# A fused forward and backward kernel on one core: the front's loads move from the SyncE queue to the GpSimd queue, and k is loaded in another order and in parts

## The chip, the cores and the metric

The kernel runs on 1 core of one Trainium2 chip. The core has five engines with queues of their own: TensorE (PE, with its weight loads PEld), VectorE (DVE), ScalarE (ACT), GpSimd (POOL) and SyncE (SP), and 16 DMA engines. Any of SP, ACT and POOL can issue a DMA. An instruction at the head of an engine's queue waits for its semaphores, and all behind it wait with it. The metric is the device time of one execution in microseconds; the median of several runs counts.

## The reference

One sequence of S = 2048 positions with D = 512 channels, F = 1376 hidden units, all bf16. The forward pass and the gradients of all inputs but `B_x` are computed.

```python
def _A_ref(q, k, v, shift_k, ssm_k, ssm_D):
    ks = shift_k.shape[-1]                      # 4
    k_pad = jnp.pad(k, ((0, 0), (ks - 1, 0), (0, 0)))
    k_shift = jnp.zeros_like(k)
    for t in range(ks):
        k_shift = k_shift + k_pad[:, t:t + S, :] * shift_k[:, ks - 1 - t][None, None, :]
    kv = k_shift * v
    ...                                         # y = kv * ssm_k, a long convolution by FFT of length 2 S
    y = y + kv * ssm_D[None, None, :]
    return q * y

def _B_ref(x, w_gate, w_up, w_down):
    ...
    return jnp.einsum("bsf,fd->bsd", g * u, w_down)

xn = _layernorm(A_q, axis=-1)
return A_q + _A_ref(xn, A_k, A_v, A_shift_k, A_ssm_k, A_ssm_D) + _B_ref(xn, B_w_gate, B_w_up, B_w_down)
...
_out, _vjp = jax.vjp(_f, ...)                   # outputs: _out and the gradients for grad_out
```

## The kernel before, in words

A position is 16 p + r: partition p holds R = 16 neighbouring rows r. Rows are worked on in eight chunks of two: chunk b is the rows 2b and 2b+1 of every partition, 128 x 2 x 512 bf16 or 256 KB. The long convolution is a Fourier transform written as matmuls with tables that the kernel makes itself (`Tables`), in two stages: `stage1` per row, then groups of 16 frequencies (`g_fwd`, `g_mul`, `g_inv`), then the inverse.

Two streams of work share the engines. `main()` is the gated layer: `ffn1(ch)` computes gate, up and the back-propagated hidden values of chunk ch (L509, L515), `yb(ch)` the two outputs (L545, L552) and adds the residual's x (`xb`, L540, used at L547). `side` is `front()` followed by `groups()`. A pacing counter takes a step of `side` after each piece of `main()`. The names in `tc.manual_schedule` and the priorities aside, the order on each engine is set by a scheduler when the program is built; at run time each engine goes through its own list in that order.

The front is what the change touches. For chunk b:
- `load_x(b)` loads x and the gradient: tiles `x_b` (4 buffers) and `go_b` (3 buffers), L300 and L305. x of chunk 5 takes the buffer of chunk 1, the gradient of chunk 4 that of chunk 1, and so on.
- `norm(b)` makes the layer norm in place: statistics and aggregates on VectorE (L323, L324), the root on ScalarE (L330), reciprocal and two rows on VectorE (L336, L339); `store_xn` writes it to memory (L347).
- `pre(b)` computes dy = gradient times xn (L380, one buffer), then ks, the sum of four shifted rows of k times the small kernel (L388, L390, L391; `ks_b` has 2 buffers and is stored at L396), and kv = ks times v (L398, in place in `v_b`, 2 buffers). dy and kv go through `stage1` (L367); ScalarE copies each result from PSUM to `fst` (L235), and L373 stores it.
- `kernel_spec()` does the same for the long kernel `ssk` in chunk 0's turn; there VectorE (L238) and ScalarE share the copies to `fst`.
- k lies in one tile `kh` of 19 rows a partition: rows 3 to 18 are the partition's own, rows 0 to 2 the three rows in front, which belong to the partition before. `load_k()` (L308) sets the first partition's front rows to zero on VectorE, loads the 2 MB of own rows, and then the front rows in two pieces (L311, L312). ks of chunk 0 reads the front rows first.

`late_loads()` calls `load_k()` and spreads the small kernel over the partitions; `front()` calls it after the first step. The tile `kh` lies where the tables' temporaries were, so it can be written when the last table has been read. Before that, the first loads (x and gradient of chunks 0 to 2, v of chunks 0 and 1, x of chunk 3, the weights) go out on SP; a part of the weights goes on ACT. In the kernel before every other load and store of the front is issued by SP too: SP's queue holds, in the scheduler's order, loads, the stores of xn, ks, fst, the hidden values `HDD`, and the DMA transposes (L491) that give `ffn1` its operands. GpSimd makes some of the tables and is then idle.

The buffers tie the loads to the work: a load into a buffer waits until the last reader of its former content is done, and stands in its queue meanwhile.

## Time and profile before

| what | value |
|---|---|
| runs | 487.74, 485.74, 487.5 us; median 487.5 |
| the profiled execution | 488.18 us, of which the span of the core is 486.3 |
| TensorE clock granted | 0.999 |
| DMA, whole span | 139.87 MB, 288 GB/s |
| stores of ks, issue to landing | 2.8 / 4.0 / 4.3 us (least, median, most) |
| loads of x (`x_b`) | 2.9 / 6.2 / 10.4 us |
| loads of the gradient (`go_b`) | 2.7 / 3.9 / 4.9 us |
| loads of v (`v_b`) | 3.1 / 4.6 / 10.2 us |
| loads of the residual's x (`xb`) | 2.8 / 3.1 / 3.9 us |

All five rows of loads and stores are of 256 KB each. In the page's tables a group of instructions stands as "busy us (x count)" per engine; in a timeline as start, duration, engine, line, operation, output<-input; in a list of waits as "who <- for whom: us in total, times, the longest". "SPq" is the queue of SP, that is the time in which it issues or waits; "issue" is time for which the profile shows no cause. In the table of stretches the columns are the stretch, its length, busy time and count of PE, PEld, DVE, ACT and POOL, the granted clock, the share of the DMA engines and GB/s. The front runs from about 25 to 120 us, the groups of frequencies from 130 to 300, the gradients of the weights and the last outputs from 300 on.

### The profile page before, as it was taken

Reading aid. Unit: us, or ns where it says so; the run is one execution under the profiler, and the core shown is the slowest. Engines: PE = TensorE matmul, PEld = TensorE weight load, DVE = VectorE, ACT = ScalarE, POOL = GpSimd, SP = SyncE. Lnnn points to the kernel's source line nnn. Section 1 sums busy time; section 2 is a strip of 40 time slices with the busy share of each in tenths; the row PEclk is TensorE's granted clock in tenths of the full one; section 3 lists DMA queues with packets and bytes.
Section 4 is the critical chain, followed back from the end, with each engine's and each line's share of the span. In section 5 each row is a group of like instructions: output and inputs, shape, how many; then the busy total and the mean of one; then the engine's idle time right before and its main releaser. Section 6 shows DMA issues by size and latency. Waiting matters only on the chain.

```text
span 486.3 us, 10468 instructions
## 1 busy us (share of the span) xinstructions
PE 468.3 (96%) x4293; PEld 314.7 (65%) x4335; DVE 340.6 (70%) x623; ACT 318.2 (65%) x354; POOL 14.0 (3%) x30
## 2 busy tenths in 40 slices
PE   8998998999999999999999999999999999999997
PEld 7876753647648547447447743576777787777875
DVE  7897979988274567686777856013266999999780
ACT  4976886859748778779779975366577535444141
POOL 8000000000000000000000000020000000000000
PEclk9999999999999999999999999999999999999999
DMA  8998998999997968968978279999999899699747
GB/s 273 375 417 307 311 247 295 353 317 330 318 296 228 267 204 259 288 199 244 296 238 268 91 288 322 387 319 309 332 349 408 285 374 413 194 266 224 207 153 249
DMA packets 105325, 139.87 MB, mean 288 GB/s; under 512 B 33307, under 2 KB 78784, under 8 KB 103742
## 3 DMA queue, kind: packets, MB, share of 16 engines
q1 hardware_dynamic: 103694, 137.84, 86.3%
q10 hardware_dynamic: 1584, 1.36, 1.0%
q8 instruction: 34, 0.56, 0.5%
q14 instruction: 13, 0.11, 0.1%
HBM read 68.45 MB, written 63.41 MB: 271 GB/s over the span
## 4 chain that ended last, share of the span: by engine, by line
PE 59%; DMA 17%; DVE 16%; SPq 3%; issue 2%; ACT 1%; ACTq 0%
PE pgu L509 13%; PE px L552 13%; PE pdh L515 6%; PE py L545 6%; PE pu L1031 6%; DMA hb<-HDD 4%; DMA Wg<-in_B_w_gate_dram 4%; DMA out_dram<-o 3%; PE ps L581 3%; PE pg L610 3%; PE pt L839 2%; PE pd L995 2%; PE pf L367 2%; DMA kh<-in_A_k_dram 2%; DVE dk L1086 2%
## 5 line engine op out<-in xcount | busy, mean ns | idle before, releaser
L552 PE MATMUL px<-WT,hd 128*128 128x512 bf16 (+1 forms) x339 | 78.6, 380 | 1.6 <-issue 1.4
L1031 PEld LDWEIGHTS <-xnC 128*128 128x128 bf16 x704 | 67.0, 98 | 8.9 <-issue 0.9
L552 PEld LDWEIGHTS <-hd 128*128 128x128 bf16 (+1 forms) x352 | 32.8, 98 | 44.2 <-issue 7.3
L1031 PE MATMUL pu<-natd,xnC 128*128 128x256 bf16 x512 | 58.5, 273 | 0.2 <-ACT nath L235 0.2
L235 ACT CAST GO<-pg 128x1024 bf16<-128x1024 f32 x48 | 46.2, 1015 | 13.4 <-issue 6.7
L597 DVE TENSOR_TENSOR T<-SP 128x2048 bf16<-128x2048 bf16 x24 | 29.3, 1222 | 34.8 <-ACT SP L235 34.8
L509 PE MATMUL pgu<-xt,Wu 128*128 128x256 bf16 (+1 forms) x352 | 53.2, 274 | 0.3
L235 ACT CAST SP<-ps 128x1024 bf16<-128x1024 f32 x48 | 46.5, 1027 | 10.3 <-PE ps L581 8.4
L509 PE MATMUL pgu<-xt,Wg 128*128 128x256 bf16 (+1 forms) x352 | 52.8, 273 | 0.3 <-DMA Wg<-in_B_w_gate_dram 0.3
L235 ACT CAST gu<-pgu 128x1024 bf16<-128x1024 f32 (+1 forms) x48 | 45.4, 945 | 11.8 <-PE pgu L509 11.3
L515 PE MATMUL pdh<-gt,WdT 128*128 128x256 bf16 (+1 forms) x352 | 46.9, 273 | 0.1
L509 PEld LDWEIGHTS <-Wu 128*128 128x128 bf16 (+1 forms) x352 | 32.9, 100 | 14.5 <-issue 9.9
L235 ACT CAST og<-pu 128x1024 bf16<-128x1024 f32 (+1 forms) x11 | 10.9, 993 | 46.8 <-PE pu L1031 28.8
L545 PE MATMUL py<-Wd,hd 128*128 128x512 bf16 (+1 forms) x168 | 40.1, 380 | 0.7 <-issue 0.5
L235 ACT CAST fst<-pf 128x1024 bf16<-128x1024 f32 x40 | 39.0, 1031 | 2.7 <-remote 1.4
L515 PEld LDWEIGHTS <-WdT 128*128 128x128 bf16 (+1 forms) x352 | 34.9, 100 | 5.4 <-ACT WdT L235 0.2
L235 ACT COPY natd<-pt 128x2048 bf16<-128x2048 bf16 x16 | 30.0, 1873 | 12.8 <-PE pt L839 12.8
L509 PEld LDWEIGHTS <-Wg 128*128 128x128 bf16 (+1 forms) x352 | 34.8, 100 | 4.2 <-DMA Wg<-in_B_w_gate_dram 0.6
L529 DVE TENSOR_TENSOR hd<-gu 128x512 bf16<-128x512 bf16 (+1 forms) x48 | 19.1, 397 | 20.7 <-ACT gu L235 20.7
L530 DVE TENSOR_TENSOR hd<-gu,dh 128x1024 bf16<-128x1024 bf16 (+1 forms) x48 | 30.8, 642 | 1.2 <-ACT dh L235 0.4
L545 PEld LDWEIGHTS <-hd 128*128 128x128 bf16 (+1 forms) x176 | 16.4, 98 | 20.5 <-issue 3.1
L597 DVE TENSOR_TENSOR U<-SP 128x2048 bf16<-128x2048 bf16 x24 | 29.2, 1217 | 0.0
(171 smaller groups left out, 696.1 us busy)
## 6 DMA issues: line engine op xcount, KB each, us to landing
HDD<-hd SPq DMA_DIRECT2D x35, 384.0 KB, 4.0
FD<-fst SPq DMA_DIRECT2D x24, 512.0 KB, 4.8
X<-FD SPq DMA_DIRECT2D x24, 512.0 KB, 5.2
GD<-GO SPq DMA_DIRECT2D x24, 512.0 KB, 3.5
g<-GD SPq DMA_DIRECT2D x12, 1024.0 KB, 8.9
hb<-HDD SPq DMA_DIRECT2D x8, 1344.0 KB, 8.4
bb<-BX SPq DMA_DIRECT2D x8, 512.0 KB, 8.6
BX<-bx SPq DMA_DIRECT2D x7, 512.0 KB, 3.9
```

The costliest lines, as they stand in the source:

```text
L235: nc.scalar.copy(o, i)
L367: nc.tensor.matmul(pf[:, c, :], lhsT=TB.W1[:, c, :], rhs=src[:, i, :], start=True, stop=not point)
L509: nc.tensor.matmul(pgu[:w, i, t, :], lhsT=W[:, c, f0:f0 + w], rhs=xt[:, :, c, :], start=(c == 0), stop=(c == NC4 - 1))
L515: nc.tensor.matmul(pdh[:w, i, :], lhsT=WdT[:, c, f0:f0 + w], rhs=gt[:, :, c, :], start=(c == 0), stop=(c == NC4 - 1))
L529: nc.vector.tensor_tensor(hd[:fw, fb0:fb0 + n, 0, :], gu[:fw, :n, 0, :], gu[:fw, :n, 1, :], op=ALU.mult)
L530: nc.vector.tensor_tensor(hd[:fw, fb0:fb0 + n, 1:3, :], gu[:fw, :n], dh[:fw, :n].unsqueeze(2).to_broadcast((fw, n, 2, 256)), op=ALU.mult)
L545: nc.tensor.matmul(py[:], lhsT=hd[:fw, fb, 0, ss], rhs=Wd[:fw, fb, :], start=(fb == 0), stop=(fb == NFB - 1))
L552: nc.tensor.matmul(px[:], lhsT=hd[:fw, fb, t, ss], rhs=W[:fw, fb, :], start=(t == 1 and fb == 0), stop=(t == 2 and fb == NFB - 1))
L581: nc.tensor.matmul(ps[32 * q:32 * q + 32, a, :], lhsT=TB.EF[64 * a:64 * a + 64, 4 * g + q, ri].rearrange("p k j -> p (k j)"), rhs=X[64 * a ...
L597: tt(W[:].rearrange("p c a d -> p c (a d)"), A[:, i:i + 1].rearrange("p c a d -> p c (a d)").to_broadcast((P, 2, 2 * D)), B[:].rearrange(" ...
L610: nc.tensor.matmul(pg[q // 2][64 * a:64 * a + 64, q % 2, :], lhsT=TB.EI[32 * q:32 * q + 32, 2 * g + a, yi].rearrange("p k c -> p (k c)"), ...
L1031: nc.tensor.matmul(pu[:, c, :, :fw], lhsT=xnC[:, r, cs(c)], rhs=nat_d(fb, r), start=(r == 0), stop=(r == R - 1))
```

## The change

Five loads are issued by GpSimd in place of SP: x from chunk 4 on, the gradient from chunk 3 on, v from chunk 2 on, all of k, and the residual's x in all eight chunks. The stores, the transposes and the first loads stay on SP. The zeros in `kh` are set by GpSimd in place of VectorE. k's front rows are issued first, then its own rows in two halves of 1 MB. `late_loads()` is called before the norm of chunk 2 in place of after it, which gives it an earlier place in the scheduler's order. What is computed and how many bytes move stay the same.

```diff
     def load_q(b):
         x = stp.tile([P, 2, D], BF, name="x_b", bufs=4)
-        nc.sync.dma_start(x[:], x_n[:, 2 * b:2 * b + 2, :])
+        (nc.sync if b < 4 else nc.gpsimd).dma_start(x[:], x_n[:, 2 * b:2 * b + 2, :])
         return x
 
     def load_go(b, x):
         go = stp.tile([P, 2, D], BF, name="go_b", bufs=3)
-        nc.sync.dma_start(go[:], go_n[:, 2 * b:2 * b + 2, :])
+        (nc.sync if b < 3 else nc.gpsimd).dma_start(go[:], go_n[:, 2 * b:2 * b + 2, :])
         XG[b] = (x, go)
 
     def load_k():
-        nc.vector.memset(ST["kh"][0:1, 0:3, :], 0.0)
-        nc.sync.dma_start(ST["kh"][:, 3:3 + R, :], k_n)
-        nc.sync.dma_start(ST["kh"][1:113, 0:3, :], k_n[0:112, R - 3:R, :])
-        nc.sync.dma_start(ST["kh"][113:128, 0:3, :], k_n[112:127, R - 3:R, :])
+        nc.gpsimd.memset(ST["kh"][0:1, 0:3, :], 0.0)
+        nc.gpsimd.dma_start(ST["kh"][1:113, 0:3, :], k_n[0:112, R - 3:R, :])
+        nc.gpsimd.dma_start(ST["kh"][113:128, 0:3, :], k_n[112:127, R - 3:R, :])
+        for r0 in range(0, R, R // 2):
+            nc.gpsimd.dma_start(ST["kh"][:, 3 + r0:3 + r0 + R // 2, :], k_n[:, r0:r0 + R // 2, :])
...
     def load_v(b):
         v = stp.tile([P, 2, D], BF, name="v_b")
-        nc.sync.dma_start(v[:], v_n[:, 2 * b:2 * b + 2, :])
+        (nc.sync if b < 2 else nc.gpsimd).dma_start(v[:], v_n[:, 2 * b:2 * b + 2, :])
         VB[b] = v
...
         xb = ybo.tile([P, 2, D], BF, name="xb", tag="xb", bufs=1)
-        nc.sync.dma_start(xb[:], x_n[:, 2 * ch:2 * ch + 2, :])
+        nc.gpsimd.dma_start(xb[:], x_n[:, 2 * ch:2 * ch + 2, :])
...
     def front():
         for b in range(8):
             if b == 0:
+                late_loads()
                 with tc.issue_after(TB.last.ins):
                     norm(2)
...
             yield
             if b == 0:
-                late_loads()
                 yield from kernel_spec()
```

In the order that is built from the changed source, TensorE's list differs from the one before only in some matmuls exchanged within the first 65 us. On VectorE the statistics, norm rows and products with k of the chunks stand earlier. On POOL the 27 DMAs stand in this order: k's front rows and halves; the residual's x of stage 0, the gradient of chunk 3, x of chunk 4; the gradient of chunk 4, x of chunk 5, v of chunk 2; the residual's x of stage 1, v of chunk 3; the gradient of chunk 5, x of chunk 6; the gradient of chunk 6, x of chunk 7, v of chunk 4; the gradient of chunk 7, v of chunks 5 and 6; the residual's x of stage 2, v of chunk 7; the residual's x of stages 3 to 7.

## The prediction

> **What bounds the kernel now.** I read first the page's busy shares and the table of stretches, then the waits of TensorE and VectorE, then the chain of waits, last the timelines where the chain leaves TensorE.

> ```profile
> PE 468.3 (96%) x4293; PEld 314.7 (65%) x4335; DVE 340.6 (70%) x623; ACT 318.2 (65%) x354; POOL 14.0 (3%) x30
> ...
> 40.00:50.00 10.00, 7.92 (x72) 6.21 (x71) 7.32 (x13) 7.33 (x10) 0.00 (x0) 1.00 0.91 287
> 70.00:80.00 10.00, 7.87 (x37) 3.48 (x36) 9.08 (x22) 5.86 (x10) 0.00 (x0) 1.00 0.80 258
> 80.00:100.00 20.00, 19.89 (x116) 11.34 (x117) 19.47 (x37) 12.89 (x17) 0.00 (x0) 1.00 0.94 329
> 100.00:120.00 20.00, 19.89 (x128) 12.51 (x129) 17.41 (x33) 16.21 (x20) 0.00 (x0) 1.00 0.92 323
> ```

> TensorE is the bound: 468.3 of 486.3 us, at full clock. Its 18.0 us of idle time lie mostly at the start, the end and two holes, in 40-50 and 70-80. From 80 to 120 it has 0.2 us left; VectorE is busy 36.9 of those 40. So the change can gain only what TensorE waits before 80, and it loses whatever makes VectorE late after 80.

> ```profile
> PE pf L367 <- DVE fst L238: 2.4, 2, 2.0
> PE pf L367 <- ACT fst L235: 2.1, 1, 2.1
> ...
> DVE ks_b L388 <- DMA KS<-ks_b: 3.7, 4, 2.0
> DVE ks_b L388 <- DMA kh<-in_A_k_dram: 3.3, 1, 3.3
> ```

> The two holes are these waits of 2.0 and 2.1 us. The chain of waits says where they come from:

> ```profile
> 34.38 0.42 SPq L311
> 34.80 0.05 issue
> 34.85 7.81 DMA kh<-in_A_k_dram
> ...
> 71.22 4.41 DMA x_b<-in_A_q_dram
> 75.66 1.28 DVE stats L323 x2
> ```

> The rows in front of k (L311, L312) are issued at 34.4 and 34.9, because the store of xn at 33.98 stands ahead of them in SP's queue and waits for the norm of chunk 2. They land at 42.66. VectorE stands 3.29 us, its copy of pf is late, TensorE waits 2.0. The second hole is another matter: x of chunk 5 is issued at 71.22, as soon as dy of chunk 1 (70.09 to 70.78) has freed its buffer. It lands at 75.63; statistics, root and two copies on ScalarE follow, and TensorE goes on at 78.97.

> ```profile
> 70.09 0.69 DVE L380 TENSOR_TENSOR dy_b<-go_b,x_b 128x1024 bf16<-128x1024 bf16 x1
> ...
> 101.51 0.69 DVE L380 TENSOR_TENSOR dy_b<-go_b,x_b 128x1024 bf16<-128x1024 bf16 x1
> ...
> 103.89 1.03 PE L367 MATMUL pf<-dy_b,W 128*128 128x512 bf16 x4
> ```

> The last two lines are dy of chunk 5: VectorE has it at 102.2, TensorE takes it at 103.89. That is the narrowest place behind 80.

> **The change, part by part.**

> *What leaves SP.* 26 issues (3 of k, 4 of x, 5 of the gradient, 6 of v, 8 of the residual's x), at 0.35 to 0.82 us each by the medians of their rows. SP also no longer stands at L540 for bx (20.1 us in 6 waits). From 160 to 280 TensorE idles only 1.3 us, so I put the relief behind the front at nothing; its ceiling is those 1.3.

> *What POOL gains.* 27 issues and the memset of k's halo. POOL has done nothing from 12.8 to 324.9 and no DMA of its own is in the trace, so the price is bounded. Issue: from 0.33 (SP's shortest) to 1.99 (SP's longest, a transpose); I take 1.02, POOL's own row on 128 partitions (tii, 4.09 for four). Landing of 256 KB: from 2.7 (the gradient's shortest) to 6.2 (the median of x); I take 3.1, the median of the residual's x, which has the same bytes and source and the least queue ahead of it. [...]

> *k.* The halo's memset can start when the last table is read (27.7); 1.37 by the row of the like memset khC gives 29.1, two issues 31.1, landing 34.2. VectorE comes to its first ks_b at about 34.0. The first half of k has until about 40. So the 3.29 us go, and with them the first hole (1.99). If k lands 4 us later than this, half of that gain is lost.

> *What VectorE does instead.* The order built from the changed source is the same on TensorE but for some matmuls exchanged before 65 us. On VectorE it is not: the norms and the k products come earlier. Between the last table (27.61) and dy of chunk 5 there now stand 2 more statistics, 2 aggregates, 2 ks_b, 2 t_b, 3 sums, a reciprocal and 2 norm rows, and the memset has gone. Back to back the timeline shows 0.60 from start to start for a product, 0.72 for the sum that needs it, 1.14 for a copy of fst, 0.33 for a norm row, 0.34 and 0.60 for the two hd, 0.12 for an aggregate. The list before adds up to 66.7, and 27.6 + 66.7 + 7.7 of waits = 102.0 against the measured 102.2, so the pitches hold. The list after adds up to 72.8: without one wait dy of chunk 5 is ready at 100.4, and 3.5 us of waits are free before TensorE stands at 103.89.

> *The waits that I count in that list* (issue 1.02, landing 3.1, and 0.35 + 4.0 for a store of ks by its medians):
> - ks_b of chunk 3 needs the store of chunk 1, 3.57 us of list behind it: 4.35 - 3.57 = 0.8.
> - x of chunk 5: dy of chunk 1 is ready at 27.6 + 40.7 + 0.8 = 69.1; then two issues (the gradient's first) and the landing, 5.14, against 3.96 of list: 1.2. It lands at 74.2, 1.4 before the 75.63 of now, so of the two holes' 4.1 us only 1.4 are gained by 79: most of what k gives is waited away here.
> - v of chunk 3 stands on POOL behind the residual's x, which waits for the second bx: 5.14 against 4.17: 1.0.
> - x of chunk 6: 0.2. x of chunk 7 behind the gradient, from dy of chunk 3: 5.14 - 3.96 = 1.2.
> - ks_b of chunk 7 needs the store of chunk 5, 3.12 of list earlier: 1.2.

> Together 5.6. dy of chunk 5 is ready at 106.0, 2.1 after TensorE wants it. TensorE's order is fixed and full behind that, so the 2.1 go to the end, and the 1.4 gained at 79 are waited away before it. v of chunk 7, behind the residual's x of stage 2 on POOL, is wanted at 120.83 and ready near 115; v of chunk 5, wanted at 109.5, is ready near 101.

> **The sum:** the profiled execution took 488.18 (span 486.3 and 1.9 around it); 488.18 + 2.1 = 490.3. The median of the runs is 0.7 lower, 487.5, so 487.5 + 2.1 = 489.6.

> Ends of the unknowns: issue 0.33 and landing 2.7 leave only the two ks waits, 2.0 us, so dy is 1.5 early: 486.0. Landing 6.2 adds 3.1 at three places, 9.3: 498.9.

> **The rivals.**

> [...]

> *Faster: the loads are early everywhere.* A queue of their own takes them past the stores (share of the DMA engines 0.91 to 1.07 from 10 to 70 us), and ks stores leave SP sooner. With no wait left in VectorE's list dy is ready at 100.4: TensorE can be 3.5 earlier, no more, so 484.0; with 1 us of waits 485.0. For it: SP's queue of 26 fewer issues. Against it: the two ks waits are the buffers', not the queue's.

> *No change:* the waits come to 3.5 and each gain is waited away at x of chunk 5 or dy of chunk 5: 486.5 to 488.5.

> **How the numbers follow.** 0.5% is 2.4 us, about what a measurement here can tell from no change: bounds 485.1 and 489.9. Forecast (486.0 to 493, likeliest 489.6) 0.45; late issues (493 to 501) 0.22; early loads (483.5 to 486) 0.18; no change 0.15. Of the forecast's chance 0.20 lies above 489.9 and 0.25 within: slower 0.42, same 0.40, faster 0.18. The forecast's own range is 487 to 493; the one that holds 8 in 10 is 484.5 to 496, which cuts the upper half of the late issues.

> **What would show it.** Right: VectorE's wait for kh under 1 us and TensorE's first hole gone; the second hole still there and longer; a new wait of pf for dy near 104; VectorE without idle time from 34 to 60. [...] Wrong: TensorE without a wait from 80 to 125, or a hole at 79 that has gone with x of chunk 5 landing before 73; then the loads are faster than my bounds. If VectorE waits for kh again, the first step has failed.

## The result, and the profile after

The changed kernel takes 500.9 us (median of 6 runs, 500.1 to 504.3) against 487.2 of the kernel before on the same chip (6 runs): a ratio of 1.0296, 95% interval [1.0261, 1.0332]. It is 13.8 us slower, where 2.1 was forecast. Its profiled execution is the slowest of the six, 504.27, with a span of 502.5 against 486.3: 16.2 longer.

The page of the changed kernel: the busy shares, and three rows of the 40 slices (each 12.6 us).

```profile
PE 478.8 (95%) x4335; PEld 317.3 (63%) x4335; DVE 340.6 (68%) x622; ACT 318.1 (63%) x354; POOL 30.3 (6%) x58
...
PEclk9999899998999999999999999999999999999999
DMA  9997995877699796978887639998999899799846
GB/s 273 375 356 196 395 273 192 293 269 271 248 314 259 247 262 212 248 240 262 249 271 249 220 104 378 314 381 283 348 329 381 291 381 392 273 214 271 256 161 204
```

VectorE and ScalarE do the same work as before (340.6 and 318.1). TensorE is idle 23.7 us (502.5 less 478.8; 18.0 before), and its clock, full in all 40 slices before, dips in slices 5 and 10. The fourth slice (37.7 to 50.2) carries 196 GB/s where its neighbours carry 356 and 395. The table of stretches, with the same columns as in the prediction, and the waits between 30 and 130 us (total, times, longest):

```profile
40.00:50.00 10.00, 7.15 (x65) 5.64 (x64) 5.49 (x10) 6.59 (x8) 0.00 (x0) 1.00 0.80 219
70.00:80.00 10.00, 9.93 (x55) 4.75 (x54) 8.73 (x14) 9.09 (x10) 1.60 (x3) 1.00 0.61 188
80.00:100.00 20.00, 14.67 (x75) 7.66 (x73) 14.39 (x31) 8.88 (x13) 3.82 (x7) 0.90 0.74 253
100.00:120.00 20.00, 17.37 (x82) 8.44 (x81) 15.74 (x30) 11.03 (x15) 1.67 (x3) 0.93 0.73 256
```

```profile
PE pf L368 <- ACT fst L235: 3.8, 2, 3.3
PE ptk L413 <- DVE fst L238: 3.6, 2, 2.5
...
PE pf L368 <- DVE dy_b L381: 2.1, 1, 2.1
...
DVE stats L324 <- DMA x_b<-in_A_q_dram: 8.8, 5, 2.6
DVE v_b L399 <- DMA v_b<-in_A_v_dram: 3.8, 2, 2.3
DVE ks_b L389 <- DMA kh<-in_A_k_dram: 2.5, 1, 2.5
```

The reader is to see three things. The first hole has not gone: VectorE waits for k again. From 80 to 120, where TensorE had 0.2 us left, it now loses 8.0. And VectorE waits mostly for x, for which the profile of before has a single wait in these 100 us:

```profile
DVE stats L323 <- DMA x_b<-in_A_q_dram: 0.9, 1, 0.9
```

The timelines of SP and GpSimd (start, duration, engine, line) show where it begins. The first two lines are of the changed kernel, the last is of the kernel before:

```profile
28.86 1.10 POOL L313 DMA_DIRECT2D kh<-in_A_k_dram  x2
...
29.41 9.68 SPq L492 DMA_TRANSPOSE gt<-go_b  x1
```

```profile
47.52 1.53 SPq L491 DMA_TRANSPOSE gt<-go_b  x1
```

The DMA transpose of chunk 2's gradient is issued at 29.41, beside k's two halves, and SP hangs in that issue for 9.68 us. Before, the same transpose was issued at 47.52, when k had landed, and its issue took 1.53. The transfers between 30 and 46 us, in 40 slices of 0.4 us (above them, in tenths, the busy share of the DMA engines):

```profile
DMA  9999998999899999211112161111111189988799
GB/s 398 403 412 435 440 406 329 412 471 490 341 449 410 413 223 138 85 73 73 73 73 90 70 75 52 56 40 56 50 56 41 38 270 328 549 287 286 278 519 306
```

From 36 to 42.8 the DMA engines carry 38 to 138 GB/s, though k is still under way: the first half, issued at 28.86, lets VectorE go on only at 44.41. Chunk 4's x, issued at 32.52, lands at 49.7. The DMA engines are not full in that stretch: from 36.4 on they are busy for one or two tenths (six in one slice), where it was eight or nine before. At dy of chunk 5, the narrow place of the prediction, it looks like this:

```profile
118.30 0.69 DVE L381 TENSOR_TENSOR dy_b<-go_b,x_b 128x1024 bf16<-128x1024 bf16 x1
...
119.04 1.26 PE L368 MATMUL pf<-dy_b,W 128*128 128x512 bf16 x4 [2.14 <-DVE dy_b L381]
```

dy is there at 118.98 instead of 102.2, and TensorE takes it 15.2 later than before; the span is 16.2 longer. So nearly the whole loss is made ahead of 120.

One more thing is in the clock column, in stretches of 2 us behind TensorE's hole of 2.54 at 53.83:

```profile
54.00:56.00 2.00, 2.00 (x19) 1.24 (x18) 2.00 (x5) 0.98 (x1) 0.00 (x0) 0.72 1.05 400
56.00:58.00 2.00, 2.00 (x10) 1.24 (x9) 2.00 (x4) 1.80 (x2) 0.00 (x0) 0.50 1.06 402
58.00:60.00 2.00, 2.00 (x19) 1.80 (x18) 1.65 (x5) 0.88 (x2) 0.00 (x0) 0.93 1.07 409
```

0.72, 0.50 and 0.93 of three times 2 us make 1.7 us of lost work: one spell of 3.4 us at half clock. There are four ahead of the end, behind the holes at 53.83 (2.54), 85.70 (3.31), 98.81 (2.02) and 119.04 (2.14), together 6.8. The rest is idle time. Before's busy row counts 4293 matmul records, this one 4335; two runs with spans of 484.7 and 484.8 (below) have 467.4 with 4293 records and 471.3 with 4335, so 3.9 us of before's idle time are missing records, and the real rise of the idle time is 5.7 + 3.9 = 9.6. 9.6 + 6.8 = 16.4, against 16.2.

### The profile page after: what moved, and what is told of

Same layout as the page of the kernel before. It is cut to its first block, busy times and chain, and to the rows that moved or that the text cites. A ratio compares the mean times of both kernels' runs of the same rounds, so it can differ in the third digit from the quotient of the medians.

```text
span 502.5 us, 10548 instructions
## 1 busy us (share of the span) xinstructions
PE 478.8 (95%) x4335; PEld 317.3 (63%) x4335; DVE 340.6 (68%) x622; ACT 318.1 (63%) x354; POOL 30.3 (6%) x58
## 4 chain that ended last, share of the span: by engine, by line
PE 62%; issue 15%; DVE 9%; DMA 8%; ACT 2%; POOL 2%; SPq 1%; POOLq 0%; DVEq 0%; ACTq 0%
PE px L553 12%; PE pgu L510 12%; PE pu L1032 10%; PE py L546 6%; PE pdh L516 6%; PE pd L996 5%; DMA out_dram<-o 3%; PE ps L582 3%; PE pg L611 2%; PE pt L840 2%; DMA bb<-BX 1%; PE po L971 1%; DMA v_b<-in_A_v_dram 1%; PE pq L913 1%; DVE dxn L1113 1%
## 5 line engine op out<-in xcount | busy, mean ns | idle before, releaser
L553 PE MATMUL px<-WT,hd 128*128 128x512 bf16 (+1 forms) x352 | 83.7, 389 | 0.0
L553 PEld LDWEIGHTS <-hd 128*128 128x128 bf16 (+1 forms) x352 | 33.6, 100 | 46.7 <-issue 11.7
L235 ACT CAST GO<-pg 128x1024 bf16<-128x1024 f32 x48 | 46.2, 1015 | 13.4 <-issue 6.7
L235 ACT CAST gu<-pgu 128x1024 bf16<-128x1024 f32 (+1 forms) x48 | 45.4, 945 | 13.3 <-PE pgu L510 12.8
L235 ACT CAST SP<-ps 128x1024 bf16<-128x1024 f32 x48 | 46.5, 1027 | 10.3 <-PE ps L582 8.4
L516 PE MATMUL pdh<-gt,WdT 128*128 128x256 bf16 (+1 forms) x352 | 48.2, 278 | 0.2 <-ACT WdT L235 0.2
L235 ACT CAST fst<-pf 128x1024 bf16<-128x1024 f32 x40 | 38.7, 1031 | 5.3 <-issue 2.7
L546 PE MATMUL py<-Wd,hd 128*128 128x512 bf16 (+1 forms) x176 | 41.5, 380 | 0.0
L516 PEld LDWEIGHTS <-WdT 128*128 128x128 bf16 (+1 forms) x352 | 35.6, 102 | 6.4 <-issue 0.5
L235 ACT CAST og<-pu 128x1024 bf16<-128x1024 f32 (+1 forms) x11 | 10.9, 993 | 44.0 <-PE pu L1032 32.9
L235 ACT COPY natd<-pt 128x2048 bf16<-128x2048 bf16 x16 | 30.0, 1874 | 13.6 <-PE pt L840 13.6
L996 PE MATMUL pd<-goC,nath 128*128 128x512 bf16 x128 | 30.1, 379 | 0.0
L546 PEld LDWEIGHTS <-hd 128*128 128x128 bf16 (+1 forms) x176 | 16.4, 98 | 20.4 <-issue 3.1
```

The source lines that it names most:

```text
L235: nc.scalar.copy(o, i)
L516: nc.tensor.matmul(pdh[:w, i, :], lhsT=WdT[:, c, f0:f0 + w], rhs=gt[:, :, c, :], start=(c == 0), stop=(c == NC4 - 1))
L546: nc.tensor.matmul(py[:], lhsT=hd[:fw, fb, 0, ss], rhs=Wd[:fw, fb, :], start=(fb == 0), stop=(fb == NFB - 1))
L553: nc.tensor.matmul(px[:], lhsT=hd[:fw, fb, t, ss], rhs=W[:fw, fb, :], start=(t == 1 and fb == 0), stop=(t == 2 and fb == NFB - 1))
L996: nc.tensor.matmul(pd[:fw, :], lhsT=nat_h(fb, r), rhs=goC[:, r, :], start=(r == 0), stop=(r == R - 1))
```

## The experiments

Eighteen versions ran, all with the same arithmetic. "Ratio" is against the kernel before on the same chip, with its 95% interval. Where "place" is said of VectorE, it is the row of an instruction in VectorE's list, in the order built from the source; equal instructions in succession count as one row.

| version | median us | ratio |
|---|---|---|
| k's order alone, on SP | 486.7 | 1.0015 [0.9985, 1.0046] |
| k part alone, on GpSimd | 495.8 | 1.0193 [1.0152, 1.0234] |
| all but the k part | 494.8 | 1.0188 [1.0121, 1.0255] |
| residual's x alone | 488.8 | 1.0035 [1.0011, 1.0059] |
| k on GpSimd, transposes held | 490.1 | 1.0066 [1.0033, 1.0100] |
| k part on ScalarE | 499.4 | 1.0259 [1.0218, 1.0300] |
| all but k, x of chunk 4 on SP | 493.1 | 1.0138 [1.0094, 1.0183] |
| all but k, every x on SP | 495.6 | 1.0169 [1.0106, 1.0233] |
| v alone | 494.0 | 1.0142 [1.0092, 1.0193] |
| gradient and residual's x | 495.1 | 1.0163 [1.0108, 1.0218] |
| whole change, transposes held | 495.4 | 1.0184 [1.0123, 1.0245] |
| k in quarters, all on SP | 486.6 | 0.9992 [0.9962, 1.0021] |
| v alone, norm of chunk 7 behind dy | 488.5 | 1.0024 [0.9990, 1.0058] |
| whole change, norms behind dy | 502.4 | 1.0300 [1.0234, 1.0365] |
| the same, transposes held | 496.1 | 1.0194 [1.0147, 1.0241] |
| kernel before, dy of chunk 5 late | 490.3 | 1.0076 [1.0047, 1.0104] |
| held, norms and ks behind dy | 490.4 | 1.0086 [1.0056, 1.0117] |
| the same, v on SP | 491.2 | 1.0090 [1.0052, 1.0128] |

### The parts alone

The first four take the change apart. k's order on SP, against the changed kernel (x, gradient, v and the residual's x go back to SP in the same way):

```diff
-        nc.gpsimd.dma_start(ST["kh"][1:113, 0:3, :], k_n[0:112, R - 3:R, :])
+        nc.sync.dma_start(ST["kh"][1:113, 0:3, :], k_n[0:112, R - 3:R, :])
...
-            nc.gpsimd.dma_start(ST["kh"][:, 3 + r0:3 + r0 + R // 2, :], k_n[:, r0:r0 + R // 2, :])
+            nc.sync.dma_start(ST["kh"][:, 3 + r0:3 + r0 + R // 2, :], k_n[:, r0:r0 + R // 2, :])
```

> All loads stay on SP, as before; of the change only the order is made (rows in front of k first, k in two halves, the block that loads k ahead of the norm of chunk 2, the halo's memset on GpSimd). Stall theory (the loss begins where GpSimd's loads of k and the DMA transpose of chunk 2's gradient run at once, 36 to 43.5 us in the changed kernel at some 65 GB/s): no such stall here, VectorE's wait for kh (3.3 before) under 1, the hole of 2.0 in 40 to 50 gone: 484.5 to 487.5. Order theory (my prediction: VectorE's list is longer because norms and k products come earlier): its list is reordered here too, so 488 to 491.

486.7, no change: as the stall theory expected. The stretch from 30 to 40 carries 379 GB/s. Two details were misjudged: the wait for kh is 2.3, not under 1, and a hole of 1.7 stays at 41.9. The run says nothing against the order theory, because VectorE's list is not reordered here as was assumed: dy of chunk 5 stands at place 176 (175 before, 189 in the changed kernel).

The k part on GpSimd, all else on SP; against the changed kernel:

```diff
-        (nc.sync if b < 4 else nc.gpsimd).dma_start(x[:], x_n[:, 2 * b:2 * b + 2, :])
+        nc.sync.dma_start(x[:], x_n[:, 2 * b:2 * b + 2, :])
...
-        nc.gpsimd.dma_start(xb[:], x_n[:, 2 * ch:2 * ch + 2, :])
+        nc.sync.dma_start(xb[:], x_n[:, 2 * ch:2 * ch + 2, :])
```

> The whole k part of the change (GpSimd, order, halves), every other load back on SP. Stall theory: k alone brings the stall, DMA under 100 GB/s for some 7 us between 35 and 45, k's halves land 14 us or more after their issue, dy of chunk 0 is taken by TensorE 5 to 6 us late, one or two spells of half clock: 493 to 497, over a third of the loss of 13.8. Queue theory (the loss is the late x and v, behind the residual's x in GpSimd's queue): the k part costs at most 2: 486 to 489.5.

495.8, as the stall theory said. Its timeline of SP, and its transfers from 30 to 46 us (slices of 0.4):

```profile
29.35 8.29 SPq L492 DMA_TRANSPOSE gt<-go_b  x1
```

```profile
GB/s 408 394 422 415 431 389 402 407 479 440 411 441 436 355 211 130 129 115 140 157 115 65 70 56 59 44 36 254 361 406 238 236 238 346 181 60 286 200 1 13
```

The same hang of SP, and 5.2 us (35.6 to 40.8) at 36 to 211 GB/s. k's halves land 14.3 after their issue (median of the two), and TensorE has a hole of 8.1 that ends at 57.1. Behind that hole stands VectorE, which waits 7.5 for x of chunk 4: its statistics have moved up in VectorE's list (place 91, 123 before), and SP issues that x only at 47.34, behind both transposes. So SP's queue, held up by the transposes, is a part of this loss beside the slow transfers.

The rest of the change with k as before, against the changed kernel:

```diff
-        nc.gpsimd.memset(ST["kh"][0:1, 0:3, :], 0.0)
...
+        nc.vector.memset(ST["kh"][0:1, 0:3, :], 0.0)
+        nc.sync.dma_start(ST["kh"][:, 3:3 + R, :], k_n)
...
```

> The change without its k part: x, gradient, v and the residual's x on GpSimd, k on SP as before. Stall theory: the transpose of chunk 2's gradient stands behind k in SP's queue again, DMA at 300 GB/s or more from 30 to 43, TensorE takes dy of chunk 0 within 1 us of before (66.1), and what is left is the late x and v between 70 and 120: 488 to 493. Queue theory: nearly the whole loss, 496 to 501.

494.8, 8.6 more than before: above what the stall theory left (488 to 493) and below what the queue theory claimed (496 to 501). There is a second cause of some size. The hole near 45 is 4.1 here: VectorE waits 4.53 for x of chunk 4.

The residual's x alone on GpSimd, against the kernel before:

```diff
-        nc.sync.dma_start(xb[:], x_n[:, 2 * ch:2 * ch + 2, :])
+        nc.gpsimd.dma_start(xb[:], x_n[:, 2 * ch:2 * ch + 2, :])
```

> Only the residual's x on GpSimd, all else as before. Both theories: SP is rid of its waits for bx (20.1 us in 6), nothing of the front is behind them: 486 to 488.5, or up to 1.3 faster (TensorE's idle time from 160 to 280). If it is slower by 3 or more, a GpSimd load beside SP's traffic costs by itself, without k and without a queue.

488.8, just above the range: 0.35% slower, interval 0.1 to 0.6. Its first load now goes out at 31 us, beside k, and k's front rows make VectorE wait 3.8 instead of 3.3; the hole of 2.5 behind it is followed by a spell of half clock.

### The stall

Holding both transposes of chunk 2 behind a store that SP has already been given, added to the version with the k part alone:

```diff
-            nc.sync.dma_start_transpose(out=t[:]...
+            with tc.issue_after(SPL[-1].ins) if ch == 2 else ExitStack():
+                nc.sync.dma_start_transpose(out=t[:]...
...
-            nc.sync.dma_start(FD[sig, :, :, r - 1:r + 1, :], st[:])
+            SPL.append(nc.sync.dma_start(FD[sig, :, :, r - 1:r + 1, :], st[:]))
```

> As the run with only the k part (495.8, on GpSimd), but both DMA transposes of chunk 2 are held behind a later store in SP's queue, so that they come where they stood before (about 45 us), with k landed. Stall theory: no stretch under 100 GB/s from 33 to 43, k's halves land within 10 us of their issue, the hole of 8.1 us in 50 to 60 is under 3: 486 to 489.5. Rival (GpSimd's loads of k are slow by themselves, or x of chunk 4, now early in VectorE's list, waits all the same): a hole of 4 or more remains, 492 to 496.

495.8 comes down to 490.1. The same stretch, 30 to 46 us:

```profile
GB/s 407 393 399 444 462 343 344 407 457 490 429 408 408 422 384 384 449 467 411 406 466 396 438 279 405 408 414 408 429 371 389 394 405 410 392 398 402 405 412 410
```

Nothing crawls, k's halves land 9.4 after their issue (median), and VectorE has no wait for kh. GpSimd still issues k; the transposes have moved to 43.7, and what stood behind them in SP's queue has moved up (x of chunk 4 from 47.34 to 36.40, and VectorE waits at most 1.2 for an x). So the stall is the meeting of transpose and k, with SP's queue standing behind it, and it costs 1.3% (1.0193 to 1.0066). 490.1 lies just above the range: a hole of 2.56 at 79.5 was not foreseen.

The same k part, issued by ScalarE:

```diff
-        nc.gpsimd.dma_start(ST["kh"][1:113, 0:3, :], k_n[0:112, R - 3:R, :])
+        nc.scalar.dma_start(ST["kh"][1:113, 0:3, :], k_n[0:112, R - 3:R, :])
...
```

> As the run with only the k part, but k's loads are issued by ScalarE instead of GpSimd; SP is as free of them, so the transpose of chunk 2's gradient again comes near 29 us, beside k. If any load beside the transpose stalls it: again some 7 us under 100 GB/s, 492 to 497. If it is GpSimd's descriptors that do not go with the transpose: the transpose's issue stays near 2 us, k's halves land within 10: 485 to 489.

```profile
GB/s 394 396 408 392 396 424 410 377 340 165 72 67 46 41 193 54 108 158 166 278 405 395 492 451 348 389 410 507 410 410 410 404 338 410 410 348 144 0 0 0
```

With no GpSimd load, the transfers crawl again, but for 4.0 us (33.6 to 37.6, at 41 to 193 GB/s) and without the hang: the transpose's issue takes 2.07, and k's first half lands 8.9 after its issue. So each theory is half right. The 499.4, above both ranges, is no price of the stall, because other things come late here: ScalarE's copies kn, for which TensorE waits 1.9 and 2.0, and a copy fst of VectorE's, for which it waits 6.9 and ahead of which VectorE had stood 4.45 for x of chunk 4. What the DMA engines do inside is left open.

### The second loss: which load?

x of chunk 4 stays on SP, in the version without the k part:

```diff
-        (nc.sync if b < 4 else nc.gpsimd).dma_start(x[:], x_n[:, 2 * b:2 * b + 2, :])
+        (nc.sync if b < 5 else nc.gpsimd).dma_start(x[:], x_n[:, 2 * b:2 * b + 2, :])
```

> As the run without the k part (494.8), but x of chunk 4 stays on SP; gradient, v, later x and the residual's x on GpSimd. Its statistics then stand behind dy of chunk 1 in VectorE's list again (place 123, as before, where the run without the k part had place 82). Theory (the early place makes VectorE stand 4.5 for a load that lands 8.4 after its issue, TensorE 4.1, and a spell of half clock costs 1.7 more): that is gone, 488 to 491. Rival (the later x and v, behind GpSimd's other waits, make the loss): 493 to 495.

493.1, in the rival's range. The theory falls: the wait for x has gone, and the hole of 3.65 at 47 is still there, because VectorE now waits 4.95 for k's front rows, which land near 44 too. What delays them, as far as these runs tell, is the early loads: with none on GpSimd VectorE waits 2.8 to 3.3 for them, with one (the residual's x, 256 KB) 3.8, with two 4.7 to 4.95; at the 400 GB/s that the slices above show from 30 to 33, 256 KB take 0.66, an estimate.

Three more versions without the k part: every x on SP; v alone on GpSimd (x, gradient and the residual's x back on SP); gradient and the residual's x on GpSimd (x and v back). Each is made of edits like these, against the changed kernel:

```diff
-        (nc.sync if b < 4 else nc.gpsimd).dma_start(x[:], x_n[:, 2 * b:2 * b + 2, :])
+        nc.sync.dma_start(x[:], x_n[:, 2 * b:2 * b + 2, :])
...
-        (nc.sync if b < 2 else nc.gpsimd).dma_start(v[:], v_n[:, 2 * b:2 * b + 2, :])
+        nc.sync.dma_start(v[:], v_n[:, 2 * b:2 * b + 2, :])
```

> As the run before it, with every x of the front on SP; gradient, v and the residual's x on GpSimd, no k part. What is left is v behind GpSimd's waits: 487.5 to 490. If x on GpSimd is harmless once chunk 4 is back, this equals the run before it within 1; if the late x of chunks 5 to 7 are the rest, it is 2 or more lower.

> Only v of the front on GpSimd, all else as before; nothing stands ahead of v in GpSimd's queue, so v is issued the moment its buffer is free. Landing theory (256 KB from GpSimd takes 5 to 6 us there, 3 to 4 from SP): VectorE waits for v at two or more places behind 80, 488.5 to 491.5. Queue theory (v is late because it stands behind the gradient's and the residual's waits on GpSimd): with v alone no wait for v over 0.5, 486 to 488.5.

> Gradient and the residual's x on GpSimd, k, x and v on SP: the run with every x on SP (495.6) less its v. If v makes the later loss, the holes from 80 to 120 go and what stays is the hole near 45 (k's front rows land at 44, because the two early GpSimd loads at 31 and 35 take their share of the full DMA engines) with its spell of half clock: 489.5 to 492. If it is not v: 494 to 496.

495.6, 494.0, 495.1: it makes little difference which of x, gradient and v leave SP (the residual's x alone had cost 0.35%). The first is above all that was expected of it, the third is where it was put if v is not the cause. v alone, which no theory priced so high, shows the place. VectorE, ScalarE and TensorE of the run with v alone:

```profile
101.22 1.29 DVE L323 BATCH_NORM_STATS2 stats<-x_b 128x6 f32<-128x512 bf16 x2 [1.62 <-DMA x_b<-in_A_q_dram]
```

```profile
103.29 0.30 ACT L330 ACTIVATE rstd<-mv,eps_t 128x2 f32<-128x2 f32 x1 [7.10 <-DVE mv L324]
...
103.96 2.84 ACT L235 CAST fst<-pf 128x1024 bf16<-128x1024 f32 x3
```

```profile
105.03 1.01 PE L367 MATMUL pf<-v_b,W 128*128 128x512 bf16 x2 [4.07 <-ACT fst L235]
```

The hole of 4.07 comes from statistics that wait for x of chunk 7, a load that is still on SP. ScalarE's root waits 7.10 for them, its three copies of pf stand behind the root, and TensorE waits 4.07 for those. VectorE's list says why (places of the statistics and of dy):

```
                         statistics of chunk 7    dy of chunk 5
kernel before                     178                  175
k's order alone, on SP            179                  176
v alone on GpSimd                 173                  181
changed kernel                    166                  189
```

With loads off SP the scheduler puts the norms of late chunks ahead of dy, for which TensorE waits. The lists show that; that it does so because it reckons with earlier loads is inferred.

### Held, and a version meant to win

The whole change with the hold of above:

> The whole change, with both DMA transposes of chunk 2 held behind a later store as in the run on k (490.1 against 495.8 without the hold). Stall theory: the same 6 us go: 493.5 to 497; the holes at 41 to 54 shrink, those behind 80 stay. Rival (the later waits swallow it, since v and x are late there whatever comes before): 498 or more.

500.9 comes down to 495.4 (1.0296 to 1.0184), as the stall theory expected; VectorE's wait for kh has gone here too.

All loads on SP, k's rows in front first, k in four pieces:

```diff
-        for r0 in range(0, R, R // 2):
-            nc.gpsimd.dma_start(ST["kh"][:, 3 + r0:3 + r0 + R // 2, :], k_n[:, r0:r0 + R // 2, :])
+        for r0 in range(0, R, R // 4):
+            nc.sync.dma_start(ST["kh"][:, 3 + r0:3 + r0 + R // 4, :], k_n[:, r0:r0 + R // 4, :])
```

> A version that may beat both: every load on SP, k's front rows first, k in four pieces instead of two, block ahead of the norm of chunk 2. The first piece lands before VectorE comes to it: its wait for kh (2.3 with halves) under 1, TensorE's hole of 1.7 near 41 gone or under 0.5: 483.5 to 486. Rival: VectorE then waits for the store of ks instead (4.1 in the run with halves) and nothing is gained: 486 to 488.

486.6, the rival's outcome: the wait for kh is 2.0, that for the store of ks 5.3. Its span is 484.8, that of k in halves on SP 484.7, against 486.3 before, but the timed runs show no difference.

### The order

The norm of chunk 7 behind dy of chunk 5, with v alone on GpSimd:

```diff
+    BEHIND = {7: 5}
...
-            elif b < 6:
-                norm(b + 2)
+            elif b < 6 and BEHIND.get(b + 2, -1) < b:
+                with tc.issue_after(DY[BEHIND[b + 2]].ins) if b + 2 in BEHIND else ExitStack():
+                    norm(b + 2)
...
-            yield from pre(b)
+            p = pre(b)
+            next(p)
+            if BEHIND.get(b + 2, -1) == b:
+                with tc.issue_after(DY[b].ins):
+                    norm(b + 2)
+            yield
+            yield from p
```

> Only v on GpSimd, as the run of 494.0, but the norm of chunk 7 is put behind dy of chunk 5 on VectorE (place 178 of dy and 179 of the statistics, as before; in the run of 494.0 the statistics stood at 173, dy at 181). Order theory (the planner, which reckons with early loads, puts the norm ahead of dy; the norm waits for x of chunk 7, ScalarE's root waits with it, and TensorE 4.1): the hole at 105 goes, 488.5 to 491.5. Landing theory (GpSimd's v lands late and that is the loss): 492.5 to 495.

494.0 becomes 488.5: the loss is gone but for 0.2% that is within the interval, with v still on GpSimd. TensorE's hole of 4.07 is now

```profile
103.08 1.04 PE L369 MATMUL pf<-dy_b,W 128*128 128x512 bf16 x4 [1.09 <-DVE dy_b L382]
```

The same in the whole change, for the norms of chunks 4, 6 and 7 (behind dy of chunks 1, 3 and 5), without and with the hold. The code is that of above but for one line:

```diff
+    BEHIND = {4: 1, 6: 3, 7: 5}
```

> The whole change, nothing held on SP; the norms of chunks 4, 6 and 7 put behind dy of chunks 1, 3 and 5 on VectorE, where they stand before. Order theory: the stall between 36 and 43 stays (6 us), of the later loss half or more goes: 493 to 497.5. Landing theory: 499 to 502.

> The whole change with both: the transposes of chunk 2 held on SP and the three norms behind their dy on VectorE; all 27 loads stay on GpSimd. If the stall and the order are the two causes, the loss nearly goes: 487.5 to 491.5. If the landing of GpSimd's loads is a third cause of size: 492 to 496.

502.4 and 496.1: the medians gain nothing, and both lie outside what the order theory gave. The traces show more. VectorE's waits for x shrink (7.9 to 1.3 with the hold), and dy of chunk 5 starts earlier than with those norms in front (111.32 after 118.30 without the hold, 108.51 after 113.05 with it), but still 7 to 10 us later than the 101.51 of before. With the hold:

```profile
108.51 0.68 DVE L383 TENSOR_TENSOR dy_b<-go_b,x_b 128x1024 bf16<-128x1024 bf16 x1
```

```profile
109.25 1.89 PE L370 MATMUL pf<-dy_b,W 128*128 128x512 bf16 x4 [4.12 <-DVE dy_b L383]
```

Without the hold the profiled execution loses most of its gain again near 406 us, where TensorE waits 4.36 for another load of k and then runs at half clock (2.19 and no spell in the changed kernel). The stall is milder in that execution, too: its page has 274 GB/s from 37.6 to 50.1 (196 in the changed kernel's fourth slice), and VectorE has no wait for kh.

The order alone, in the kernel before, with every load on SP; `N7[-1]` is the last norm row of chunk 7, so dy of chunk 5 goes behind it:

```diff
-        nc.vector.tensor_tensor(dy[:], go[:], xn[:], op=ALU.mult)
+        with tc.issue_after(N7[-1].ins) if b == 5 else ExitStack():
+            nc.vector.tensor_tensor(dy[:], go[:], xn[:], op=ALU.mult)
```

> The kernel before, all loads on SP, with dy of chunk 5 put behind the norm of chunk 7 on VectorE (dy at place 186 and the statistics at 177; 175 and 178 before). Order theory: x of chunk 7 lands near 104 there, dy comes at 107 instead of 101.5, TensorE stands some 3.5 near 104 and runs a spell of 3.4 us at half clock behind it: 490.5 to 493.5 with no load on GpSimd at all. Landing theory: nothing changes, 486.5 to 488.5.

490.3, just under the range: a hole of 2.31 at 109.3 and a spell of half clock, without one load on GpSimd. Order alone makes a loss of 0.8%.

Then the list of the version with hold and norms was compared with that of the kernel before once more: all products ks of chunk 6 and the first of chunk 7 stand ahead of dy of chunk 5. So these went behind too, and beside it v went back to SP:

```diff
+    KSB = {6: 5, 7: 6}
...
         for n, j in enumerate((3, 2, 1, 0)):
+            with tc.issue_after(DY[KSB[b]].ins) if b in KSB else ExitStack():
...
```

> The version of 496.1 (whole change, transposes held, three norms behind dy, all 27 loads on GpSimd), with the products ks of chunks 6 and 7 also put behind dy of chunks 5 and 6, where they begin before; in the version of 496.1 six of them (some 0.6 each) stand ahead of dy of chunk 5, and dy is ready at 108.5, TensorE waits 4.1 for it near 105 and then runs 3.4 us at half clock. Order theory: dy some 3.6 earlier, that hole under 1 and its half clock gone: 489 to 492.5. Landing theory (v lands late from GpSimd, and dy waits behind the v products all the same): 493.5 to 497.

> The same with v back on SP (k, gradient, x and the residual's x on GpSimd). If the landing of GpSimd's v is what remains, 1.5 or more under the run beside it: 487.5 to 490.5. If order was all, equal to it within 1.5.

490.4, as the order theory gave it, and 491.2, equal within 1.5. With all 27 loads on GpSimd, hold and order together take the change from 1.0296 to 1.0086; v on SP adds nothing. In the first of the two:

```profile
105.15 0.69 DVE L403 TENSOR_TENSOR v_b<-ks_b,v_b 128x1024 bf16<-128x1024 bf16 x1 [5.84 <-DMA v_b<-in_A_v_dram]
...
105.76 0.68 DVE L384 TENSOR_TENSOR dy_b<-go_b,x_b 128x1024 bf16<-128x1024 bf16 x1
```

dy of chunk 5 is ready at 106.4, 2.8 earlier than without the last edit. In front of it a product waits for a v that GpSimd issued at 98.83, right behind a gradient that had waited for dy; on SP the same v went out at 98.91, behind a store. 0.9% of the loss remains, and what makes it is not settled.

## Why the prediction was wrong

*The sign was right, the mechanism in part, the size far off: 489.6 forecast (484.5 to 496), 500.9 measured.*

*The step that failed first is "What leaves SP", where I "put the relief behind the front at nothing".* I counted the issues and waits that SP is rid of, looked for what they free behind the front, and did not ask what then comes first in SP's queue within the front. It is the DMA transpose of chunk 2's gradient, which in the kernel before stood behind k. It met k's halves, and both crawled. Cost: 1.1% of the 3.0% (1.0296 to 1.0184 with the hold).

*k, "the first half of k has until about 40".* The front rows came when I had said, at 34.4 against 34.2, but by luck: they were issued by 28.9, not 31.1, and took 6.0 from issue to landing, not 3.1. The half came at 44.4. My sign of failure, "If VectorE waits for kh again, the first step has failed", is what the trace shows: 2.52. With the transposes held that wait is not there, so it comes from what moved up in SP's queue.

*Issue, taken as 1.02: mis-sized.* GpSimd issues a load in 0.54 (median; the first in 0.82, all others in 0.53 to 0.63), also between 80 and 120, and VectorE's products stay at 0.69. My bounds for it were misread: SP's issues in the profile of before go from 0.24 to 7.48, not from 0.33 to 1.99, and the longest are transposes of the last part (5.76 to 7.48), a row that could have warned of them. No run shows the late issues to which the chances give 0.22: in their place stand the 0.54 and the 0.69, and that the measured time lies in their range (493 to 501) is luck.

*Landing, taken as 3.1, at most 6.2: mis-sized early, mostly in bounds later.* Behind 50 us the medians are 5.1 for v (4.2 before) and 4.7 for the gradient (4.4); the longest were a gradient with 6.8 and an x with 7.3. Among the early loads k's halves took 16.6 (median) and chunk 4's x 17.1. v's median is 0.9 later than before, but with hold and order put back v on SP left the time unchanged, so where v is issued is no cause of size.

*VectorE's list to dy of chunk 5, "66.7" to "72.8": right, and undervalued.* Without a wait dy would have been ready at 100.4; I counted 5.6 of waits, and it was ready at 118.98, so there were 18.6. The list itself came out as added up; the waits were mis-sized. The six places that I had counted at 5.6 took 8.7 (x of chunk 7 alone 2.60, counted as 1.2). Another 8.9 came at places that I had not counted: x of chunk 3 (1.39) and of chunk 4 (1.99), k (2.52), the store of ks that chunk 2 needs (1.43) and v of chunk 5 (1.52). I had not asked of each instruction that had moved up whether its input would be there, such as the statistics of chunk 4 (place 91, before 123). The new wait of pf for dy came, as forecast, but at 119 and not at 104. Cost of the order: 1.0% (1.0184 to 1.0086, with the hold in place; the whole order was not put back without the hold).

*The working let a hole of TensorE cost its own length (the 2.1 "go to the end"): too little here.* Four of them were each followed by a spell that lost 1.7 us, 6.8 of the 16.2 in the profiled run. They are part of the two costs above, not beside them.

*The rivals.* "Faster" falls: the loads that started early, at 28.9 to 32.5, landed at 44.4 to 49.7. "No change" falls, too: the waits came to 18.6, not to 3.5. The second hole did stay and grow, as forecast (2.13 to 3.31).

*Left open:* the last 0.9% [0.6, 1.2], and why transpose and loads crawl together.

## What to carry to other kernels

Loads that leave an in-order queue let what stood behind them start early: look at what that is and what it meets, a DMA transpose above all (here its meeting with k cost 1.1 to 1.3%). Where a scheduler makes the lists, moving loads to another queue can re-sort the lists of the engines that use them; compare where the one instruction stands for which the bound engine waits, and ask of each one that moved ahead of it when its input really lands. Taking all the loads and then undoing them one by one was misleading here, since every subset with x, the gradient or v in it put late statistics ahead of dy; putting the order back while the loads stayed moved was what told the causes apart.
